# Gated mix of linear-memory attention and a ReGLU block: memory retrieval with phi(Q) stationary, and an order written out per engine

## Chip, cores and metric

One core of one Trainium2 chip. The metric is the device time of one launch in microseconds. The kernel before was run three times: 268.81, 269.09 and 269.09 us, median 269.09.

## What is computed

Inputs are x (2048 tokens by 512, bf16), attention weights wq, wk, wv, wo (512 by 512), one gate beta per head, the weights of a ReGLU block (512 by 1792 twice, 1792 by 512), and a gate vector. Attention has 32 heads of 16 and works in 4 segments of 512 tokens; a memory M (16 by 16 per head) and a denominator vector z are carried from segment to segment.

```python
phi = lambda t: jnp.where(t > 0, t + 1.0, jnp.exp(t))
for s in range(N):                       # 4 segments of 512 tokens
    p = softmax(qs @ ks.T * scale + mask)
    a_dot = p @ vs
    num = einsum('bhld,bhde->bhle', phi(qs), M)
    den = einsum('bhld,bhd->bhl', phi(qs), z) + 1e-06
    o = g * num / den + (1.0 - g) * a_dot         # g = sigmoid(beta), per head
    M = M + einsum('bhld,bhle->bhde', phi(ks), vs)
    z = z + phi(ks).sum(over tokens)
a = o @ wo
b = (relu(x @ W_gate) * (x @ W_up)) @ W_down
out = gx * a + (1 - gx) * b                       # gx = sigmoid(sum(x * gate_w)), per token
```

In segment 0 the memory is empty, so retrieval (num and den) is computed in segments 1 to 3 only.

## The kernel before

**Data.** Activations lie transposed: `xT`, `QT`, `KT`, `pqT` (phi of Q) and `oT` have features on 128 partitions, in 4 blocks of 128 features (8 heads each), and 512 tokens along the row. The hidden layer `hT` has 14 blocks. All weights stay in SBUF. `xT` is double-buffered; segments 1 to 3 are brought in by a DMA transpose on the sync queue (SP, L352). The buffer `xT[1]` first serves to stage segment 0, which TensorE (PE) transposes itself (L404).

**Attention in a segment.** For each pair of feature blocks nine QK steps (L738) each fill the four banks of the PSUM tile `sp`; ScalarE (ACT) takes the exponential (L749) and GpSimd (POOL) masks the diagonal (L759). A step PV (L808) multiplies with the values for one feature block; VectorE (DVE) transposes the result 32 by 32 (L826), takes the reciprocal of the softmax sums (L831), multiplies with gates (L834) and with the product (L837), adds the memory's part (L842) and transposes back into `oT` (L859).

**Memory.** For a finished segment, phi(K) is transposed by DMA (`pkT` to `pK`, L352 as well), multiplied with the values (L650), accumulated in `mzacc`, and spread into `mnum` (a block-diagonal 128 by 128 per feature block) and `mden` (128 by 8) by L668 and L671. In the next segment:

- ZD (L687): 16 matmuls with a tile of phi(Q) as weights and 8 columns of `mden` streaming give the denominators, tokens on partitions. DVE adds 1e-6 (L694) and takes the reciprocal (L697); POOL multiplies with the gates (L700, L703) and copies the result into the layout `coefM` in 48 small copies (L711).
- MR (L779): one matmul per feature block with `mnum` as weights and 512 columns of phi(Q) streaming gives the numerators, features on partitions. DVE transposes them (L786), DVE or POOL multiplies with `coefM` (L792), and the sum with the softmax part follows in L842.

**The rest.** Per segment 14 pairs of gate and up products (L918) with relu (L930 or L932) and product (L937), then four output rows of down product (L952) and wo (L965) in the same bank, scaled out of PSUM (L974 or L976) and stored. The last output row is cut into three column pieces (L876, L884). The head gates are computed once, near the start, by L434 to L437.

**PSUM banks.** Apart from `sp` there are four banks `rb`, shared by all other products: a step takes a bank, and the step that reads it out gives it back.

**Order.** All work is recorded as steps in a `Plan`, with engine, cost, latency, dependencies and a due time. `lay_out` walks through modelled time and on each free engine starts the ready step with the smallest due time, shifted by the tables `SHIFT` and `NUDGE`; a bank is chosen in the same walk. The emission order of each engine is the result; on the chip every engine works through its list in order and waits on semaphores. Two DMA issues are moved to another step's place by `issue_with` (L997).

Of the kernel before, what the change touches and what calls it, by code (L numbers as in the profile page):

```python
# [8 lines left out]
BF16 = mybir.dt.bfloat16  # L9
F32 = mybir.dt.float32  # L10
# [24 lines left out]
NCH = 2  # L35

SHIFT = {'PA': 15, 'PB': 0, 'LIKE': 35, 'T': -43, 'PQ': 42, 'N': -104, 'MZ': -228, 'PV': -136, 'OS': -150, 'OC': -94, 'R': -63, 'EX': -241, 'QK': -81, 'KC': 5, 'H': -95, 'KTR': -235, 'TG': -121, 'PK': -281, 'VC': -64, 'MN': 30, 'XC': 118, 'MK': 208, 'K': -25, 'U': 10, 'D': 11, 'EK': 57, 'MQ': 24, 'EQ': -42, 'TR': 201, 'MA': -36, 'KO': 124, 'V': -15, 'G': 8, 'QC': 201, 'KX': 50, 'W': 72, 'Q': -21, 'OX': 45, 'TA': -65, 'GS': 41, 'TL': -45, 'TN': 103, 'TB': 8, 'MR': 0}
KEEP = {'D': 2, 'U': 1, 'Q': 2, 'G': 1, 'V': 1, 'MZ': 1}  # L40
SWITCH = 0.094
NUDGE = [
# [57 lines left out]
T0, TU, SPAN, PEN_D, PEN_A, PEN_P = 19.0, 15.6, 4.1, -23.0, 150.0, 146.0  # L100


PORT = {'KO', 'MB', 'MQ', 'MN', 'GS', 'PQ', 'PK', 'N1', 'N2', 'N3', 'NM'}
PIECE = {'MK': 0.445, 'TL': 0.22, 'ZE': 0.24, 'YL': 0.22, 'MB': 0.3}


# [934 lines left out]
```

## Time and profile before

| what | value |
|---|---|
| runs | 268.81, 269.09, 269.09 us |
| the profiled execution | 268.84 us, of which the span from first to last instruction is 267.1 us |
| busy, share of the span | PE 97%, ACT 72%, DVE 69%, POOL 61% |
| ACT L749 (exponentials) | 72 of 1876 ns |
| POOL L759 (masks) | 256 of 443 ns |
| DVE L937 (hidden product) | 56 of 684 ns |
| DVE L786 (transpose of the retrieved numerators) | 12 of 700 ns |
| DVE L842 and POOL L842 (sum of both parts) | 18 of 428 ns, 6 of 754 ns |
| POOL L711 (copies into `coefM`) | 48 of 243 ns |

An entry "72 of 1876 ns" is a group of instructions of one source line: count and mean length. Lengths of neighbouring instructions on one engine can overlap, because an engine may start one before the one ahead has left its pipeline. A "wait" or "idle before" names what released the engine.

### The profile page before, as it was taken

The page shows a single profiled execution, that of the slowest core. Times are in us where ns is not written, and L with a number is a line of the kernel's source. Part 1 is how long each engine was busy: PE and PEld are TensorE (multiplying, and loading weights), DVE is VectorE, ACT ScalarE, POOL GpSimd, SP SyncE. Part 2 cuts the span into 40 slices and gives each one's busy share as a digit, 9 for nine tenths or more (in the row PEclk, how much of TensorE's full clock was granted, in tenths as well). Part 3 has the DMA queues.
Part 4 walks back from the last instruction along what each step waited for, and adds up shares of the span by engine and source line. Part 5 has one row for each costly group of instructions (what it writes and reads, how often), then busy time and mean ns, then how long its engine had stood idle before and what let it go on. Part 6 is the DMA issues. An engine that isn't in the chain of part 4 may idle for free.

```text
span 267.1 us, 8000 instructions
## 1 busy us (share of the span) xinstructions
PE 258.6 (97%) x3322; PEld 120.8 (45%) x3365; DVE 185.4 (69%) x414; ACT 192.3 (72%) x185; POOL 163.5 (61%) x378
## 2 busy tenths in 40 slices
PE   7999999999999999999999999999999999999995
PEld 5544544444454444444445544444444444444444
DVE  1476898798589956995858758896816545878800
ACT  3789999987789876687978867666559757876021
POOL 8435788557888874644884888644425785645400
PEclk9999999999999999999999999999999999999999
DMA  6996682221203210000210000000020000000011
GB/s 202 338 345 143 119 281 25 46 57 35 51 28 75 49 38 22 2 2 0 59 22 25 21 22 0 23 4 0 2 64 20 25 0 22 0 4 2 2 39 39
DMA packets 26292, 15.06 MB, mean 56 GB/s; under 512 B 13584, under 2 KB 26256, under 8 KB 26256
## 3 DMA queue, kind: packets, MB, share of 16 engines
q1 hardware_dynamic: 25904, 14.29, 19.6%
q8 instruction: 26, 0.43, 0.6%
q10 hardware_dynamic: 288, 0.26, 0.3%
q14 instruction: 10, 0.08, 0.1%
q0 software_dynamic: 64, 0.00, 0.0%
HBM read 8.13 MB, written 2.10 MB: 38 GB/s over the span
## 4 chain that ended last, share of the span: by engine, by line
PE 92%; issue 2%; POOL 2%; DMA 1%; ACT 1%; DVE 1%; SPq 0%; DVEq 0%; POOLq 0%
PE rb L918 36%; PE rb L952 16%; PE rb L491 10%; PE sp L738 9%; PE rb L808 7%; PE rb L965 5%; PE rb L533 4%; DMA wv_sb<-in_A_wv_dram 1%; PE rb L876 1%; PE rb L779 1%; PE rb L516 1%; POOL E L759 1%; ACT E L749 1%; POOL mnum L668 1%; DVE tA L826 0%
## 5 line engine op out<-in xcount | busy, mean ns | idle before, releaser
L749 ACT ACTIVATE E<-sp 128x2048 bf16<-128x2048 f32 x72 | 135.1, 1876 | 34.5 <-PE sp L738 32.9
L759 POOL TENSOR_SCALAR_AFFINE_SELECT E<-E 64x256 bf16<-64x256 bf16 x256 | 113.4, 443 | 74.6 <-ACT E L749 62.3
L918 PE MATMUL rb<-xT,wg_sb 128*128 128x512 bf16 x214 | 55.0, 380 | 0.6
L918 PE MATMUL rb<-xT,wu_sb 128*128 128x512 bf16 x212 | 54.7, 380 | 0.8 <-issue 0.3
L937 DVE TENSOR_TENSOR hT<-rb,rg 128x512 bf16<-128x512 f32 x56 | 38.1, 684 | 23.3 <-PE rb L918 14.6
L952 PE MATMUL rb<-wd_sb,hT 128*128 128x512 bf16 x198 | 47.0, 379 | 1.6 <-issue 1.4
L918 PEld LDWEIGHTS <-wg_sb 128*128 128x128 bf16 x224 | 20.4, 98 | 26.2 <-issue 4.3
L918 PEld LDWEIGHTS <-wu_sb 128*128 128x128 bf16 x224 | 20.6, 98 | 25.2 <-issue 3.0
L952 PEld LDWEIGHTS <-hT 128*128 128x128 bf16 x210 | 19.3, 98 | 24.6 <-issue 3.5
L738 PE MATMUL sp<-QT,KT 16*64 16x320 bf16 (+7 forms) x512 | 30.3, 295 | 0.1
L738 PE MATMUL sp<-QT,KTo 32*64 32x320 bf16 (+7 forms) x512 | 30.3, 295 | 0.0
L930 ACT ACTIVATE rg<-rb 128x512 bf16<-128x512 f32 x35 | 20.8, 595 | 8.8 <-PE rb L918 7.0
L826 DVE STREAM_TRANSPOSE tA<-rb 128x512 f32<-128x512 f32 x32 | 20.8, 689 | 7.0 <-PE rb L808 7.0
L738 PEld LDWEIGHTS <-KT 16*64 16x64 bf16 x512 | 10.6, 102 | 28.3 <-issue 28.3
L974 ACT ACTIVATE osb<-rb,ngcol 128x512 bf16<-128x512 f32 x11 | 7.5, 685 | 15.9 <-PE rb L965 15.9
L808 PE MATMUL rb<-E,Vs 64*32 64x448 bf16 (+7 forms) x512 | 18.8, 284 | 0.0
L808 PE MATMUL rb<-E,Vp 64*32 64x448 bf16 (+7 forms) x512 | 18.4, 284 | 0.0
L491 PE MATMUL rb<-xT,wq_sb 128*128 128x512 bf16 x63 | 16.3, 380 | 0.1
L491 PE MATMUL rb<-xT,wk_sb 128*128 128x512 bf16 x60 | 15.9, 379 | 0.2
L932 DVE TENSOR_SCALAR rg<-rb 128x512 bf16<-128x512 f32 x21 | 14.2, 683 | 1.3 <-PE rb L918 0.7
L965 PE MATMUL rb<-wo_sb,oT 128*128 128x512 bf16 x57 | 14.4, 379 | 0.5 <-issue 0.5
L389 DVE CAST QT<-rb 128x512 bf16<-128x512 f32 x11 | 7.6, 689 | 9.4 <-PE rb L491 9.4
(107 smaller groups left out, 313.9 us busy)
## 6 DMA issues: line engine op xcount, KB each, us to landing
out_dram<-osb SPq DMA_DIRECT2D x15, 128.0 KB, 1.7
wd_sb<-in_B_W_down_dram SPq DMA_DIRECT2D x1, 1792.0 KB, 8.0
wg_sb<-in_B_W_gate_dram SPq DMA_DIRECT2D x3, 512.0 KB, 7.0
wu_sb<-in_B_W_up_dram SPq DMA_DIRECT2D x3, 512.0 KB, 8.5
Vs<-Vp SPq DMA_DIRECT2D x8, 144.0 KB, 3.2
wk_sb<-in_A_wk_dram SPq DMA_DIRECT2D x2, 256.0 KB, 3.9
wq_sb<-in_A_wq_dram SPq DMA_DIRECT2D x2, 256.0 KB, 4.7
wo_sb<-in_A_wo_dram SPq DMA_DIRECT2D x1, 512.0 KB, 8.8
```

What stands on the lines that cost most here:

```text
L491: nc.tensor.matmul(rb[s.bank][:], lhsT=w[:, ci, c * P:(c + 1) * P], rhs=xT[i][:, ci, :], start=(ci == 0), stop=(ci == NC - 1))
L738: nc.tensor.matmul(sp[64 * h:64 * h + 64, j, off:off + m], lhsT=kt[32 * j:hi, c0 + w, 64 * ck:64 * ck + 64], rhs=QT[i][32 * j:hi, c0 + w, ...
L749: nc.scalar.activation(Er[n % NE][:], sp[:], ACT.Exp, scale=SCALE)
L759: nc.gpsimd.affine_select(out=v, in_=v, compare_op=ALU.is_ge, fill=0.0, base=0, pattern=[[0, 4], [1, 64]], channel_multiplier=-1)
L808: nc.tensor.matmul(rb[s.banks[h]][32 * j:32 * j + 32, q0:q0 + m], lhsT=v[64 * h:64 * h + 64, ck // 2, o:o + 32], rhs=Er[(base + f) % NE][6 ...
L826: nc.vector.transpose(tA[k].rearrange("p b w -> p (b w)"), rb[a.banks[r]][:])
L918: nc.tensor.matmul(rb[s.bank][:], lhsT=w[:, ci, fv * P:(fv + 1) * P], rhs=xT[i][:, ci, :], start=(ci == 0), stop=(ci == NC - 1))
L930: nc.scalar.activation(rgb[k][:], rb[a.bank][:], ACT.Relu)
L932: nc.vector.tensor_scalar(rgb[k][:], rb[a.bank][:], 0.0, None, ALU.max)
L937: nc.vector.tensor_tensor(hT[:, fv, :], rb[a.bank][:], rgb[k][:], ALU.mult)
L952: nc.tensor.matmul(rb[b][:], lhsT=hT[:, fv, lc:lc + P], rhs=wd_sb[:, fv, :], start=(fv == 0), stop=False)
L965: nc.tensor.matmul(rb[hold.bank][:], lhsT=oT[i][:, ci, lc:lc + P], rhs=wo_sb[:, ci, :], start=False, stop=(ci == NC - 1))
```

## The change

Retrieval is turned round, and the way the order is made is replaced.

- `mnum` and `mden` become one tile `mem` of 136 columns per feature block. `retrieve` takes the place of `coefficients`: for each of the 16 combinations of 128 tokens and one feature block, the phi(Q) tile is the stationary operand and the 136 columns stream. Numerators and denominators arrive together, tokens on partitions. Six MR steps per segment hold 3, 3, 3, 3, 2 and 2 of these matmuls in one bank each.
- A step RN follows each MR on DVE: add 1e-6, reciprocal, multiply with `gr` (head gate times token gate, one POOL operation per segment), multiply the numerators into `mtok`.
- Four DMA transposes MX per segment on the sync queue bring `mtok` into `memT` (features on partitions).
- The sum with the softmax part is now OA, an addition into `oT` after the second transpose (L859), on DVE or POOL. L786, L792 and L842 are gone; L837 writes `o16` directly.
- `ORDER` lists the steps of each of PE, ACT, DVE, POOL and SP in sequence; `lay_out` follows the lists and still chooses banks. `SHIFT`, `KEEP`, `NUDGE` and `issue_with` are gone. The order on every engine differs from the one before; among other things the transpose of segment 1's x is issued after the first weight load, and relus and evacuations are divided anew between ACT and DVE.
- The first two shifts of V wait for six weight loads, and the load of wo, like that of W_down, waits for segment 0's phi(K) transposes.

```diff
+RW = P + 8
-NUDGE = [
...
+ENGINES = ('PE', 'ACT', 'DVE', 'POOL', 'QSP')
+ORDER = [
...
+        for v in ORDER:
+            queues[ENGINES[v % len(ENGINES)]].append(self.steps[v // len(ENGINES)])
...
+        while len(order) < len(self.steps):
+            best = None
+            for e in line:
+                if at[e] == len(queues[e]):
+                    continue
+                s = queues[e][at[e]]
+                if s.left or s.take > len(free):
+                    continue
+                t = max(free_at[e], s.ready, free[s.take - 1][0] if s.take else 0.0)
+                if best is None or t < best[0]:
+                    best = t, e, s
...
-    mnum = [sb([NC, P], BF16, f"mnum{i}") for i in range(2)]
-    mden = [sb([NC, 8], BF16, f"mden{i}") for i in range(2)]
-    dinv = sb([4, H], F32, "dinv")
-    coefM = [sb([NC, NB, 2], F32, f"coefM{i}") for i in range(2)]
+    mem = [sb([NC, RW], BF16, f"mem{i}") for i in range(2)]
+    gr = sb([4, NC, 8], F32, "gr")
+    rcf = [sb([3, 8], F32, f"rcf{i}") for i in range(2)]
+    mtok = sb([4, D], BF16, "mtok")
+    memT = sb([NC, L], BF16, "memT")
...
+        def z2(e, s):
+            nc.gpsimd.tensor_tensor(gr[:], gcat[:, None, :, 1, :].to_broadcast([P, 4, NC, 8]),
+                                    rcol[:, 4 * seg:4 * seg + 4, None, None].to_broadcast([P, 4, NC, 8]), ALU.mult)
+        g = add(f"ZC{seg}", {"POOL": 0.5}, z2, after=[hrow, d["TE"]] + recs, prio=want - 20.0)
+        d["MX"] = []
+        cuts = (0, 3, 6, 9, 12, 14, 16)
+        for q in range(6):
+            ks = range(cuts[q], cuts[q + 1])
+
+            def mrv(e, s, ks=ks):
+                for n, k in enumerate(ks):
+                    t, c = divmod(k, NC)
+                    nc.tensor.matmul(rb[s.bank][:, RW * n:RW * n + RW], lhsT=pqT[i][:, c, t * P:(t + 1) * P], rhs=mem[o][:, c, :],
+                                     start=(n == 0), stop=(n == len(ks) - 1), skip_group_check=True)
+            mr = add(f"MR{seg}{q}", {"PE": 0.061 * len(ks)}, mrv, after=d["PQ"] + st[seg - 1]["mb"], prio=want + 4.0 * q,
+                     take=True, lat=0.25)
+            d["mr"].append(mr)
+
+            def rn(e, s, ks=ks, mr=mr, q=q):
+                n, f = len(ks), rcf[q % 2]
+                b = rb[mr.bank][:, 0:RW * n].rearrange("p (n w) -> p n w", n=n)
+                nc.vector.tensor_scalar(f[:, 0:n], b[:, :, P:], 1e-6, None, ALU.add)
+                nc.vector.reciprocal(f[:, 0:n], f[:, 0:n])
+                nc.vector.tensor_tensor(f[:, 0:n], f[:, 0:n], gr.rearrange("p t c h -> p (t c) h")[:, ks[0]:ks[-1] + 1], ALU.mult)
+                nc.vector.tensor_tensor(mtok.rearrange("p t (c h v) -> p (t c) h v", c=NC, h=8)[:, ks[0]:ks[-1] + 1],
+                                        b[:, :, 0:P].rearrange("p n (h v) -> p n h v", h=8),
+                                        f[:, 0:n, :, None].to_broadcast([P, n, 8, DH]), ALU.mult)
+            recs.append(add(f"RN{seg}{q}", {"DVE": 0.42 + len(ks) * P / 960.0}, rn,
+                            after=[mr, g] + (st[seg - 1]["MX"] if seg > 1 else []), prio=want + 4.0 * q, give=mr))
             for t in range(4):
+                if ks[0] <= 4 * t + 3 <= ks[-1]:
+                    d["MX"].append(transpose(f"MX{seg}{t}", memT[:, :, t * P:(t + 1) * P], mtok[:, t, :],
+                                             recs[-2:] + oadd[-NC:], want + 4.0 * q, 128))
...
-                chain = [n1, n2, n3, n4] if seg else [n1, n2, n3]
+                chain = [n1, n2, n3]
...
+            if seg:
+                def oa(e, s, c=c):
+                    eng = nc.gpsimd if e == "POOL" else nc.vector
+                    eng.tensor_tensor(oT[i][:, c, :], oT[i][:, c, :], memT[:, c, :], ALU.add)
+                b = add(f"OA{seg}{c}", {"DVE": 0.34, "POOL": (1.1, PEN_P)}, oa, after=[b, *d["MX"]], prio=want, lat=0.2)
+                oadd.append(b)
```

More of the change, by code (lines that the diff above doesn't have):

```diff
@@ L125, in add @@
         kind = name.rstrip("_0123456789") if name[0] != "N" else "N"
-        s.name, s.lat, s.prio, s.emit = name, lat, prio + SHIFT.get(kind, 0.0), emit
+        s.name, s.lat, s.prio, s.emit = name, lat, prio, emit
         s.engines = {e: (c if isinstance(c, tuple) else (c, 0.0)) for e, c in engines.items()}
         s.after = [a for a in after if a is not None]
-        s.take, s.give, s.keep, s.mode = int(take), give, KEEP.get(kind, 0), mode
+        s.take, s.give, s.keep, s.mode = int(take), give, 0, mode
         s.followers, s.start, s.bank, s.which = [], None, None, which
@@ L136, in lay_out @@
     def lay_out(self):
+        line, queues = sorted({e for s in self.steps for e in s.engines}, key=self.first), {}
+        for e in line:
+            queues[e] = [s for s in self.steps if list(s.engines) == [e]] if e not in ENGINES else []
+        for v in ORDER:
+            queues[ENGINES[v % len(ENGINES)]].append(self.steps[v // len(ENGINES)])
         for s in self.steps:
             s.left, s.ready = len(set(s.after)), 0.0
-            s.prio += NUDGE[s.seq] / 10.0 if NUDGE else 0.0
@@ L140, in lay_out @@
             for a in set(s.after):
                 a.followers.append(s)
-        waiting = [s for s in self.steps if s.left == 0]
-        events = [(0.0, -1, None, None)]
-        n = 0
-        free_at = {e: 0.0 for s in self.steps for e in s.engines}
-        now, done, order, mode = 0.0, 0, [], "full"
-        pool = sorted(self.banks)
-        gp, lock = (0.0, 0.0, 99.0), 0.0
-        while done < len(self.steps):
-            if not events:
-                raise RuntimeError("plan stuck: " + ", ".join(s.name for s in waiting[:8]))
-            now = events[0][0]
-            while events and events[0][0] <= now + 1e-9:
-                _, _, what, s = heapq.heappop(events)
-                if what == "done":
-                    if s.give is not None:
-                        pool.extend(s.give.banks[n_] for n_ in s.which or range(len(s.give.banks)))
-                    for f in s.followers:
-                        f.left -= 1
-                        if f.left == 0:
-                            waiting.append(f)
-            going = True
-            while going:
-                going = False
-                for e in free_at:
-                    if free_at[e] > now + 1e-9:
-                        continue
-                    best = held = None
-                    here = []
-                    for s in waiting:
-                        if e in s.engines:
-                            key = (s.prio + s.engines[e][1] - (SHIFT.get("LIKE", 0) if e == "PE" and s.mode != "full" != mode else 0.0), s.seq)
-                            if not s.take or len(pool) >= s.keep + s.take:
-                                here.append((key, s))
-                            elif s.take > 1 and (held is None or key < held):
-                                held = key
-                    for key, s in here:
-                        if held is not None and s.take and key > held:
-                            continue
-                        if best is None or key < best_key:
-                            best, best_key = s, key
-                    if best is None:
-                        continue
-                    waiting.remove(best)
-                    best.start = (now, len(order), e)
-                    if best.take:
-                        best.banks = [pool.pop(0) for n_ in range(best.take)]
-                        best.bank = best.banks[0]
-                    cost = best.engines[e][0]
-                    if e == "PE":
-                        cost += SWITCH if best.mode != mode else 0.0
-                        mode = best.mode
-                    if e == "DVE" and best.port:
-                        if now < gp[1]:
-                            rest = min(gp[0] + (int((now - gp[0]) / gp[2]) + 1) * gp[2], gp[1]) - now
-                            cost += max(0.0, rest - 0.14)
-                        lock = now + cost
-                    elif e == "POOL":
-                        cost += max(0.0, lock - now)
-                        gp = (now, now + cost, best.piece)
-                    free_at[e] = now + cost
-                    n += 1
-                    heapq.heappush(events, (now + cost, n, "free", None))
-                    n += 1
-                    heapq.heappush(events, (now + cost + best.lat, n, "done", best))
-                    order.append(best)
-                    done += 1
-                    going = True
@@ new lines, in lay_out @@
+        at, free_at = {e: 0 for e in line}, {e: 0.0 for e in line}
+        free = [(0.0, b) for b in self.banks]
+        gp, lock, mode, order = (0.0, 0.0, 99.0), 0.0, "full", []
+        while len(order) < len(self.steps):
+            best = None
+            for e in line:
+                if at[e] == len(queues[e]):
[6 more added lines that the diff above has]
+                    best = t, e, s
+            if best is None:
+                raise RuntimeError("plan stuck")
+            now, e, s = best
+            cost = s.engines[e][0]
+            if s.take:
+                s.banks = [b for _, b in free[:s.take]]
+                s.bank = s.banks[0]
+                del free[:s.take]
+            if e == "PE":
+                cost += SWITCH if s.mode != mode else 0.0
+                mode = s.mode
+            if e == "DVE" and s.port:
+                if now < gp[1]:
+                    rest = min(gp[0] + (int((now - gp[0]) / gp[2]) + 1) * gp[2], gp[1]) - now
+                    cost += max(0.0, rest - 0.14)
+                lock = now + cost
+            elif e == "POOL":
+                cost += max(0.0, lock - now)
+                gp = (now, now + cost, s.piece)
+            free_at[e] = now + cost
+            done = now + cost + s.lat
+            s.start = (now, len(order), e)
+            order.append(s)
+            at[e] += 1
+            if s.give is not None:
+                for n in s.which or range(len(s.give.banks)):
+                    free.append((done, s.give.banks[n]))
+                free.sort(key=lambda f: f[0])
+            for f in s.followers:
+                f.ready = max(f.ready, done)
+                f.left -= 1
@@ L209, in lay_out, with first @@
         self.order = order
         return max(s.start[0] for s in order)
+    def first(self, e):
+        return next(s.seq * 64 + list(s.engines).index(e) for s in self.steps if e in s.engines)
 def act(n, sbuf=False):
@@ L335, with dma @@
     add = plan.add
[L338 removed]
+    def dma(eng, o, i, after=(), prio=0.0, kb=512, lat=3.0, name="dma"):
         key = {"SP": nc.sync, "ACT": nc.scalar, "POOL": nc.gpsimd}[eng]
@@ L465, in sh @@
                                   in_=Vp[i][64 - 64 * h:128 - 64 * h, :, VR * h:VR * h + VR])
-            d["VS"].append(add(f"VS{seg}{h}", {"QSP": 0.65}, sh, after=d["V"] + prev, prio=t_unit(seg, 0) - 2.0, lat=2.2))
+            d["VS"].append(add(f"VS{seg}{h}", {"QSP": 0.65}, sh, after=d["V"] + prev + ([ld[f"{w}{n}"] for w in ("wg", "wu") for n in range(3)] if seg == 0 else []), prio=t_unit(seg, 0) - 2.0, lat=2.2))
     def t_unit(seg, c):
@@ L677, in memory, with retrieve @@
         d["mb"] = [add(f"MB{seg}", {"DVE": 0.95, "POOL": (2.05, 60.0)}, mb, after=[m] + rd, prio=want)]
-    def coefficients(seg):
+    def retrieve(seg):
         i, d, o = seg % 2, st[seg], (seg - 1) % 2
-        want = t_unit(seg, 0)
-        def zd(e, s):
-            for t in range(4):
-                for c in range(NC):
-                    nc.tensor.matmul(rb[s.bank][:, H * t + 8 * c:H * t + 8 * c + 8], lhsT=pqT[i][:, c, t * P:(t + 1) * P],
-                                     rhs=mden[o][:, c, :], start=(t == 0 and c == 0), stop=(t == 3 and c == NC - 1),
-                                     skip_group_check=True)
-        z = add(f"ZD{seg}", {"PE": 16 * 0.027}, zd, after=d["PQ"] + st[seg - 1]["mb"], prio=want, take=True, lat=0.25)
-        d["mr"].append(z)
-        def z0(e, s):
-            nc.vector.tensor_scalar(dinv[:], rb[z.bank][:, 0:4 * H].rearrange("p (t h) -> p t h", t=4), 1e-6, None, ALU.add)
-        def z1(e, s):
-            nc.vector.reciprocal(dinv[:], dinv[:])
-        def z2(e, s):
-            nc.gpsimd.tensor_tensor(dinv.rearrange("p t (c h) -> p t c h", c=NC),
-                                    dinv.rearrange("p t (c h) -> p t c h", c=NC),
-                                    gcat[:, None, :, 1, :].to_broadcast([P, 4, NC, 8]), ALU.mult)
-            nc.gpsimd.tensor_tensor(dinv[:], dinv[:], rcol[:, 4 * seg:4 * seg + 4, None].to_broadcast([P, 4, H]), ALU.mult)
-        b = add(f"ZA{seg}", {"DVE": 0.25}, z0, after=[z] + (st[seg - 1]["CF"] if seg > 1 else []), prio=want, give=z)
-        b = add(f"ZB{seg}", {"DVE": 0.88}, z1, after=[b], prio=want)
-        b = add(f"ZC{seg}", {"POOL": 0.9}, z2, after=[b, hrow, d["TE"]], prio=want)
-        d["CF"] = []
-        for q in range(4):
-            def z3(e, s, q=q):
-                for j in range(4):
-                    nc.gpsimd.tensor_copy(coefM[i][32 * j:32 * j + 32].rearrange("p c (t q) r -> p c t q r", q=4)[:, :, :, q, :],
-                                          dinv[32 * q:32 * q + 32].rearrange("p t (c h) -> p c t h", c=NC)[:, :, :, 2 * j:2 * j + 2])
-            d["CF"].append(add(f"ZE{seg}{q}", {"POOL": 0.95}, z3, after=[b] + (st[seg - 2]["cr"] if seg > 2 else []), prio=want))
@@ L774, in attend @@
                 fill(seg, c)
-            os_, mem = [], []
-            if seg >= 1:
-                def mrv(e, s, c=c):
-                    nc.tensor.matmul(rb[s.bank][:], lhsT=mnum[(seg - 1) % 2][:, c, :], rhs=pqT[i][:, c, :],
-                                     start=True, stop=True)
-                mr = add(f"MR{seg}{c}", {"PE": mm(L)}, mrv, after=d["PQ"][c:c + 1] + st[seg - 1]["mb"] + mems[-2:][:1] * (len(mems) > 1),
-                         prio=tu + 0.8 * TU, take=True, lat=0.25)
-                d["mr"].append(mr)
-                def tm(e, s, mr=mr, u=u):
-                    nc.vector.transpose(tM[u % 2].rearrange("p b r e -> p (b r e)"), rb[mr.bank][:])
-                t = add(f"TM{seg}{c}", {"DVE": dve(L)}, tm, after=[mr] + mems[-2:][:1] * (len(mems) > 1),
-                        prio=tu + 0.8 * TU, lat=0.15, give=mr)
-                def n3m(e, s, c=c, u=u):
-                    eng = nc.gpsimd if e == "POOL" else nc.vector
-                    eng.tensor_tensor(om[u % 2][:], tM[u % 2][:],
-                                      coefM[i][:, c, :, :, None].to_broadcast([P, NB, 2, DH]), ALU.mult)
-                mem = [add(f"NM{seg}{c}", {"DVE": dve(L), "POOL": (1.1, PEN_P)}, n3m,
-                           after=[t, *d["CF"]] + (sums[-2] if len(sums) > 1 else []), prio=tu + 0.85 * TU, lat=0.15)]
-                mems.append(mem[0])
-                d["cr"].append(mem[0])
-            adds = []
+            os_ = []
             want = tu + TU * 0.95
@@ L813, in attend @@
             pp = a = add(f"PV{seg}{c}", {"PE": 1.02}, pv, mode="cols2",
-                         after=[masks[base + f] for f in need] + d["V"] + d["VS"] + mems[-2:][:1],
+                         after=[masks[base + f] for f in need] + d["V"] + d["VS"],
                          prio=want, take=2, lat=0.3)
@@ L859, in t2 @@
                 nc.vector.transpose(oT[i][:, c, :], o16[u % 2].rearrange("p b r e -> p (b r e)"))
-            d["oT"].append(add(f"TB{seg}{c}", {"DVE": dve(L)}, t2, after=os_ + wr, prio=want - 10.0, lat=0.2))
-            otr.append(d["oT"][-1])
-    fills, readers, masks, kph, kts, otr, chains, pvs, mems, sums = [], {}, {}, [], [], [], [], [], [], []
+            b = add(f"TB{seg}{c}", {"DVE": dve(L)}, t2, after=os_ + wr, prio=want - 10.0, lat=0.2)
+            otr.append(b)
+            if seg:
[4 more added lines that the diff above has]
+                oadd.append(b)
+            d["oT"].append(b)
+    fills, readers, masks, kph, kts, otr, chains, pvs, recs, oadd = [], {}, {}, [], [], [], [], [], [], []
     rgn, rgu, sts = [0], [], []
@@ L990 @@
             if seg == 0:
-                ld["wd"].after += st[0]["PK"]
+                for w in ("wd", "wo"):
+                    ld[w].after += st[0]["PK"]
         else:
@@ L995 @@
         st[seg]["readers_xT"] = st[seg]["xr"]
-    def issue_with(step, host, first):
-        own, hosts = step.emit, host.emit
-        step.emit = lambda e, s: None
-        def both(e, s):
-            for fn in (own, hosts) if first else (hosts, own):
-                fn(e, s)
-        host.emit = both
-    issue_with(ld["wu1"], ld_x[1], True)
-    issue_with(ld["wo"], ld["wd"], False)
     plan.makespan = plan.lay_out()
```

31 lines of the change are left out of this document (10 added, 21 removed), and 111 rows, old and new, of tables (NUDGE, ORDER).

## Prediction

> **What bounds the kernel now.** I read the busy shares first, then what TensorE waited for, then the chain that ended last.
>
> ```profile
> PE 258.6 (97%) x3322; PEld 120.8 (45%) x3365; DVE 185.4 (69%) x414; ACT 192.3 (72%) x185; POOL 163.5 (61%) x378
> ```
>
> ```profile
> PE rb L952 <- issue: 1.4, 9, 0.2
> PE rb L394 <- DVE zeros L265: 1.1, 1, 1.1
> PE rb L404 <- DMA xT<-in_A_x_dram: 0.5, 1, 0.5
> PE rb L965 <- issue: 0.5, 3, 0.2
> PE rb L918 <- issue: 0.3, 2, 0.2
> ```
>
> A busy PE alone proves little, because pipelined matmuls overlap. The second view proves it: in 267.1 us PE waited 1.1 us for the first memset, 0.5 us for the first load, and otherwise only for "issue". No wait for VectorE (DVE), ScalarE (ACT) or GpSimd (POOL) is left after the first few microseconds. So the time is the sum of PE's own steps. A microsecond of PE work taken out is worth a microsecond; DVE or POOL work taken out is worth nothing by itself; and whatever makes PE wait is paid in full. The granted clock is 1.00 in every stage.
>
> **PE's work.** These pieces of the chain give the prices (start, length, line, matmuls):
>
> ```profile
> 144.36 0.38 PE rb L687 x16
> ...
> 260.04 1.53 PE rb L876 x14
> ...
> 262.01 0.78 PE rb L876 x14
> ```
>
> L687 (denominators, 8 columns) takes 0.38 us for 16, three times: 1.1 us, removed. L779 (retrieval, 512 columns) has 12 matmuls at 0.216 us, the spacing of the 512-column matmuls (8 in 1.73 us in the same view): 2.6 us, removed. Added are 48 matmuls of 136 columns, each with weights of its own. L876 does just that: a fresh hT tile for each matmul, 0.78/14 = 55.7 ns at 128 columns, 1.53/14 = 109 ns at 256. So 136 columns cost 59 ns, and 48 of them 2.8 us. PE's net is 1.1 + 2.6 - 2.8 = **0.9 us less**. In the built order the changes between full-array and tiled matmuls number 164 in both kernels, so they cancel.
>
> The Trainium skill, "TensorE: Matmul & The Clock Gate", section on the back-to-back issue gap, speaks against this: in a stream of weight loads and matmuls it gives about 81 ns for N=128, and calls the short gap that of an isolated matmul. By it the 48 would take 3.9 us or more and PE would gain nothing. The L876 row, a stream with a load for every matmul, does not agree; I take the row.
>
> **DVE's work, where the change can lose.** Gone from DVE: L786 8.4, L842 7.4, its share of L792 5.1, L697 2.8, L694 0.9: 24.6 us. From POOL: L711 11.7, L792 5.8, L842 4.5, L700 and L703 2.6. None was waited for by PE, so this gains nothing directly. Added on DVE are 18 normalisation steps RN (add 1e-6, reciprocal, times the gate, then the wide multiply out of PSUM) and 10 of the 12 additions OA into oT. The new order also moves work from ACT: relus on DVE go from 21 to 34, output scalings from 5 to 10, Q evacuations from 11 down to 5.
>
> The four operations of an RN depend on one another, and each waits for DVE's own semaphore in the built program. What such a wait costs is visible at the head gates, L434 to L437 (start, length):
>
> ```profile
> 7.46 0.18 DVE L434 TENSOR_SCALAR gbt<-eb 128x32 f32<-128x32 f32 x1
> 7.68 0.35 DVE L435 RECIPROCAL gb<-gbt 128x32 f32<-128x32 f32 x1
> 8.07 0.18 DVE L436 COPY gcat<-gb 128x32 f32<-128x32 f32 x1
> 8.16 0.18 DVE L437 TENSOR_TENSOR gcat<-eb,gb 128x32 f32<-128x32 f32 x1
> ```
>
> L437 needs nothing of L436 and starts 0.09 us after it, inside it. L435 needs L434 and starts 0.22 us after it, 0.04 us behind its end. A dependent operation pays its whole length plus about 0.03 us. The later timeline agrees:
>
> ```profile
> 207.51 0.29 DVE L694 TENSOR_SCALAR dinv<-rb 128x128 f32<-128x128 f32 x1 [1.11 <-PE rb L687]
> 207.84 0.95 DVE L697 RECIPROCAL dinv<-dinv 128x128 f32<-128x128 f32 x1
> 208.71 0.65 DVE L826 STREAM_TRANSPOSE tA<-rb 128x512 f32<-128x512 f32 x1
> ```
>
> L697 starts 0.33 us after L694; the independent L826 starts inside L697.
>
> So an RN on 24 denominators costs: add 0.18 (0.18 at 32 elements in L434), reciprocal 0.29 (between 0.22 at 16 elements in L831 and 0.35 at 32), gate 0.18 (0.19 in L834 and L437), each plus 0.03: 0.74. The wide multiply of 384 PSUM elements lies between L837 (256 elements, 0.38 at the shortest) and L937 (512, 0.69), less the 0.08 that the next instruction overlaps: 0.47. That is **1.2 us**, and by the same rows 1.0 us for the two-piece RN (16 denominators, 256 elements). The plan that the order was built for books 0.42 + 0.13 a piece: 0.82 and 0.69. Its 0.42 fits independent operations, not a chain. Missing: 12 x 0.38 + 6 x 0.31 = 6.4 us. Ends: nothing if the slack holds it all, 6.4 us if each RN releases what PE waits for.
>
> The Trainium skill, "VectorE: DVE Perf Modes", section on the DRAIN, says that the next operation waits for the pipe to empty anyway and that the semaphore costs nothing extra. The rows above do not agree: 0.22 us with the dependence, 0.09 us without. By the page the plan's figure would be right, which is the first rival below.
>
> **Where it bites.** An RN gives back the PSUM bank of its product MR, and only four such banks exist. At the turn from segment 0 to 1 the built order has on PE: MR (2 matmuls), MR (3), MR (3), the second half of a down product (L952, 7), MR (2), a QK, then three K projections (L491, 4 matmuls each). The down product holds one bank throughout, so the last MR needs the first RN's bank and the three K projections need those of the second, third and fourth. On DVE stand RN, a small reciprocal, RN, RN, a small multiply, RN. Counting from the first MR, PE wants the first K at 0.12 + 0.18 + 0.18 + 7 x 0.216 + 0.12 + 0.45 = 2.6 us. DVE starts at about 0.4 (0.22 matmul length in the L876 row, the second matmul, a semaphore), so the second RN ends at 0.4 + 1.0 + 0.15 + 1.2 = 2.75, and its bank is free at about 2.95 (0.08 of tail, 0.1 of semaphore): 0.35 late. The second K is wanted at 2.95 + 0.93 = 3.9, free at 4.15: 0.25. The third is wanted at 5.0, free at 0.4 + 1.0 + 0.15 + 1.2 + 1.2 + 0.1 + 1.0 + 0.2 = 5.25 to 5.3: 0.3. Together **0.9 us**. With the plan's figures the fourth RN ends at 3.85 and nothing is late. The order decides at a mean RN of about 0.88 us; I have 1.1, the plan 0.75.
>
> Five other RNs stand directly ahead of a product that takes their bank or share its queue (one just before this place, two around the last QK blocks of segment 2, two in segment 3): 5 x 0.38 = 1.9 us at stake. DVE in such stretches is already full (busy 9.67 of 10 us from 50 to 60, 17.3 of 20 from 160 to 180), so I take half: **1.0 us**, bounds 0 and 1.9.
>
> **DMA and the rest, at nothing.** Twelve DMA transposes MX join the sync queue (SP), like the present pK ones: 1.2 us of issue, 2.7 us (2.3 to 4.2) to landing. OA waits for them and the output product W for OA. Between the last PV and the first W of the last segment stand five products of PE, 6.8 us, over a DVE chain of about 5; without that cover an OA is 0.4 us late. SP's first transpose of x moves ahead of all weight loads but one, and the second K product of PE after the first QK now needs it.
>
> ```profile
> xT<-in_A_x_dram SPq DMA_TRANSPOSE x3, 5.5
> ```
>
> The three took 3.9, 5.5 and 9.0 us, the 9.0 behind queued weights. It can start at about 8.3, when its staging tile has been read (last L404), and is wanted at about 15.6: it lands at 12.2 to 17.3. I take 0, since only one 256 KB weight load stands ahead of it; at most 1.7 us late. Weight loads that now stand behind pK transposes have several QK blocks of 3 us before their use.
>
> **Sum.** 268.84 (this profiled execution: span 267.1 and 1.7 around it) - 0.9 + 0.9 + 1.0 = 269.8. The runs' median is 0.25 above the profiled run, so I say **269.9 us**.
>
> **Rivals.**
> - *The RNs cost what the plan says, or slack hides them*: only PE's gain is left, 268.84 - 0.9 = 267.9. This is the other side, faster. It decides at the bank hand-over above, at a mean RN below 0.88 us. For it: PE in the kernel before, laid out by the same kind of plan, waits for nobody. Against it: the L434 to L437 rows. The DRAIN section of "VectorE: DVE Perf Modes" in the Trainium skill would give this result.
> - *The new matmuls do not stream*: if each 98 ns weight load (the L876 load row) is exposed, 48 x 98 = 4.7 us replaces 2.8, so PE has 1.0 more instead of 0.9 less, and with the RN waits 271.7. The page on TensorE in the Trainium skill leans this way; the L876 spacing is against it.
> - *The early transpose is late*: 1.7 on top, 271.5.
> - *The RN excess reaches PE in full*: 268.84 - 0.9 + 6.4 = 274.3, from 271.5 up.
>
> **Chances.** Forecast (268.6 to 271.2) 0.55; RN cheap or hidden (267.5 to 268.5) 0.23; exposed weight loads 0.05; late transpose 0.07; excess in full 0.10. The range from 267.6 to 272.0 leaves out most of the last case and a little of the others. A measurement here can tell about 0.2%, 0.54 us, from no change. Faster by more (under 268.55) is the second case, 0.23; within it (to 269.63) is the low part of the forecast, 0.17; slower is the rest, 0.60.
>
> **What would show it.** Right: L687-like small matmuls gone, the new MR at about 59 ns spacing, the RN chain with 0.03 us gaps and 1.0 to 1.2 us a step, and PE's waits naming DVE (the RN multiply) ahead of K projections at 65 to 72 us. Wrong: RN steps under 0.9 us, PE with no wait for DVE, MR spacing near 98 ns, or a wait of the first segment-1 projection for the DMA of xT.

## The result and the profile after

The changed kernel takes 270.47 us (median of 6 runs, 270.07 to 270.70), the kernel before 268.92 us on the same chip (6 runs, 268.72 to 269.09). The ratio is 1.0056, with a 95% interval of 1.0043 to 1.0069: slower by about 0.6%. The profiled execution took 270.44 us with a span of 268.7 us. The forecast was 269.9 us, in the right direction and 0.6 us short.

The busy shares of the profile after:

```profile
PE 261.7 (97%) x3353; PEld 121.2 (45%) x3353; DVE 189.7 (71%) x462; ACT 184.3 (69%) x175; POOL 140.4 (52%) x319
```

POOL lost 23 us of work and ACT 8, DVE gained 4, and none of this says anything about the time. PE's busy time can't be compared across the two pages either: before, 43 matmul records are missing beside the 3365 weight loads, here none. What PE waited for tells more (in total, times, longest, in us), in the kernel after:

```profile
PE rb L473 <- DVE mtok L690: 1.2, 3, 0.5
...
PE rb L882 <- DVE mtok L690: 0.4, 1, 0.4
PE rb L678 <- DVE mtok L690: 0.4, 1, 0.4
```

The lines left out are waits for the first memset and the first loads (1.8 us in all). Before, PE waited for nobody after the start (the view stands in the prediction). Now three lines name L690, the wide multiply that ends a step RN and gives its PSUM bank back: K projections (L473), a hidden product (L882) and a retrieval product MR (L678). PE's timeline shows the first of them, at the turn from segment 0 to 1 (start, length, line, matmuls, idle time before):

```profile
66.48 0.65 PE L678 MATMUL rb<-mem,pqT 128*128 128x136 bf16 x8
66.97 1.67 PE L916 MATMUL rb<-wd_sb,hT 128*128 128x512 bf16 x7
68.48 0.28 PE L678 MATMUL rb<-mem,pqT 128*128 128x136 bf16 x2
...
69.65 1.02 PE L473 MATMUL rb<-xT,wk_sb 128*128 128x512 bf16 x4 [0.54 <-DVE mtok L690]
71.08 1.02 PE L473 MATMUL rb<-xT,wk_sb 128*128 128x512 bf16 x4 [0.41 <-DVE mtok L690]
72.32 1.02 PE L473 MATMUL rb<-xT,wk_sb 128*128 128x512 bf16 x4 [0.21 <-DVE mtok L690]
```

This is the order that the prediction worked with: four MR, a down product that holds one bank, and three K projections, each of which must wait for the RN of the bank it takes. DVE's timeline of the same stretch (left out: the third RN's reciprocal and the first three operations of the fourth, 71.14 to 71.81):

```profile
66.81 0.17 DVE L687 TENSOR_SCALAR rcf<-rb 128x16 f32<-128x16 f32 x1
67.02 0.25 DVE L688 RECIPROCAL rcf<-rcf 128x16 f32<-128x16 f32 x1
67.31 0.27 DVE L689 TENSOR_TENSOR rcf<-rcf,gr 128x16 f32<-128x16 f32 x1
67.61 0.42 DVE L690 TENSOR_TENSOR mtok<-rb,rcf 128x256 bf16<-128x256 f32 x1
67.96 0.24 DVE L794 RECIPROCAL co<-tA 128x16 f32<-128x16 f32 x1
68.14 0.18 DVE L687 TENSOR_SCALAR rcf<-rb 128x24 f32<-128x24 f32 x1
68.36 0.30 DVE L688 RECIPROCAL rcf<-rcf 128x24 f32<-128x24 f32 x1
68.70 0.31 DVE L689 TENSOR_TENSOR rcf<-rcf,gr 128x24 f32<-128x24 f32 x1
69.04 0.56 DVE L690 TENSOR_TENSOR mtok<-rb,rcf 128x384 bf16<-128x384 f32 x1
69.52 0.17 DVE L687 TENSOR_SCALAR rcf<-rb 128x24 f32<-128x24 f32 x1
...
70.06 0.38 DVE L689 TENSOR_TENSOR rcf<-rcf,gr 128x24 f32<-128x24 f32 x1
70.47 0.56 DVE L690 TENSOR_TENSOR mtok<-rb,rcf 128x384 bf16<-128x384 f32 x1
70.95 0.17 DVE L797 TENSOR_TENSOR co<-co,Gs 128x16 f32<-128x16 f32 x1
...
71.84 0.42 DVE L690 TENSOR_TENSOR mtok<-rb,rcf 128x256 bf16<-128x256 f32 x1
```

In this stretch each operation of an RN starts 0.03 to 0.04 us after the end of the one ahead (66.81 + 0.17 = 66.98, next 67.02). Independent neighbours overlap: L794 starts at 67.96, inside L690, which ends at 68.03. From their first start to the start of what follows, the four RNs took 1.15, 1.38, 1.43 and 1.05 us. The three releases of PE (69.65, 71.08, 72.32) follow the ends of the second, third and fourth L690 (69.60, 71.03, 72.26) by 0.05 to 0.06 us: DVE sets PE's pace here.

**How the stalls are counted.** The idle times in brackets begin at a matmul's modelled end, but starts can be compared across kernels. In what follows a *stall* is the spacing from a matmul's start to the next beyond the shortest spacing that the same pair of steps shows in any of these traces, summed from 11.5 us on. (A pair that only one kernel has can show no stall this way; the wait view has to serve for those.) The kernel before has 0.00 us. The kernel after has 2.68 us: 0.43 at the MR that starts at 61.29, 1.56 at the three K projections, 0.09 near 181.6, and 0.60 at hidden products at 224 to 226. Taking the stall away from the stretch from the first QK to the last matmul leaves 248.52 us before and 247.32 us after. So PE's own work fell by 1.2 us and its waits grew by 2.7 us; the difference of 1.5 us is what the runs show (270.47 - 268.92 = 1.55).

### The profile page after: what moved, and what is told of

Same layout as the page of the kernel before. It is cut to its first block, busy times and chain, and to the rows that moved or that the text cites. A ratio compares the mean times of both kernels' runs of the same rounds, so it can differ in the third digit from the quotient of the medians.

```text
span 268.7 us, 8009 instructions
## 1 busy us (share of the span) xinstructions
PE 261.7 (97%) x3353; PEld 121.2 (45%) x3353; DVE 189.7 (71%) x462; ACT 184.3 (69%) x175; POOL 140.4 (52%) x319
## 4 chain that ended last, share of the span: by engine, by line
PE 91%; DVE 6%; DMA 2%; issue 1%; SPq 0%; DVEq 0%
PE rb L882 35%; PE rb L916 17%; PE rb L473 10%; PE sp L723 9%; PE rb L771 7%; PE rb L929 5%; PE rb L515 4%; DMA wv_sb<-in_A_wv_dram 2%; DVE mtok L690 1%; PE rb L840 1%; PE rb L498 1%; PE rb L678 1%; DVE rcf L688 1%; DVE rcf L689 1%; PE rb L632 1%
## 5 line engine op out<-in xcount | busy, mean ns | idle before, releaser
L744 POOL TENSOR_SCALAR_AFFINE_SELECT E<-E 64x256 bf16<-64x256 bf16 x256 | 111.3, 435 | 91.6 <-ACT E L734 78.3
L882 PE MATMUL rb<-xT,wg_sb 128*128 128x512 bf16 x224 | 56.0, 380 | 0.4 <-DVE mtok L690 0.4
L882 PE MATMUL rb<-xT,wu_sb 128*128 128x512 bf16 x224 | 55.9, 380 | 0.0
L916 PE MATMUL rb<-wd_sb,hT 128*128 128x512 bf16 x210 | 49.9, 380 | 0.0
L882 PEld LDWEIGHTS <-wg_sb 128*128 128x128 bf16 x224 | 20.5, 98 | 25.2 <-issue 4.1
L882 PEld LDWEIGHTS <-wu_sb 128*128 128x128 bf16 x224 | 20.2, 98 | 25.1 <-issue 4.9
L896 DVE TENSOR_SCALAR rg<-rb 128x512 bf16<-128x512 f32 x34 | 23.1, 679 | 6.6 <-PE rb L882 6.2
L789 DVE STREAM_TRANSPOSE tA<-rb 128x512 f32<-128x512 f32 x32 | 22.1, 701 | 7.9 <-PE rb L771 7.3
L894 ACT ACTIVATE rg<-rb 128x512 bf16<-128x512 f32 x22 | 12.8, 598 | 9.2 <-PE rb L882 9.2
L473 PE MATMUL rb<-xT,wk_sb 128*128 128x512 bf16 x64 | 16.3, 379 | 1.2 <-DVE mtok L690 1.2
L473 PE MATMUL rb<-xT,wq_sb 128*128 128x512 bf16 x64 | 16.3, 380 | 0.0
L938 ACT ACTIVATE osb<-rb,ngcol 128x512 bf16<-128x512 f32 x6 | 4.1, 686 | 17.2 <-PE rb L929 17.1
L371 DVE CAST Vp<-rb 128x256 bf16<-128x256 f32 (+1 forms) x18 | 8.4, 474 | 10.5 <-PE rb L515 9.3
L929 PE MATMUL rb<-wo_sb,oT 128*128 128x512 bf16 x60 | 15.3, 380 | 0.0
```

What stands on the lines that cost most here:

```text
L473: nc.tensor.matmul(rb[s.bank][:], lhsT=w[:, ci, c * P:(c + 1) * P], rhs=xT[i][:, ci, :], start=(ci == 0), stop=(ci == NC - 1))
L744: nc.gpsimd.affine_select(out=v, in_=v, compare_op=ALU.is_ge, fill=0.0, base=0, pattern=[[0, 4], [1, 64]], channel_multiplier=-1)
L789: nc.vector.transpose(tA[k].rearrange("p b w -> p (b w)"), rb[a.banks[r]][:])
L882: nc.tensor.matmul(rb[s.bank][:], lhsT=w[:, ci, fv * P:(fv + 1) * P], rhs=xT[i][:, ci, :], start=(ci == 0), stop=(ci == NC - 1))
L894: nc.scalar.activation(rgb[k][:], rb[a.bank][:], ACT.Relu)
L896: nc.vector.tensor_scalar(rgb[k][:], rb[a.bank][:], 0.0, None, ALU.max)
```

## The experiments

The theory is that of the prediction: the RN is a chain of dependent operations on DVE, longer than the plan booked, and PE pays where banks are handed over. Rivals: the chain costs nothing by itself and PE is slower for another reason (weight loads, the transposes, the new order as a whole); or the added DVE work as such is the price.

| kernel | RN with 24 / 16 denominators, us | stall, us | median (runs), us | ratio to before (95%) |
|---|---|---|---|---|
| after | 1.36 / 1.07 | 2.68 | 270.47 (6) | 1.0056 (1.0043 to 1.0069) |
| without the chain | 0.85 / 0.63 | 0.00 | 267.73 (6) | 0.9952 (0.9939 to 0.9966) |
| one more link | 1.58 / 1.30 | 4.36 | 272.35 (4) | 1.0127 (1.0114 to 1.0141) |
| one link fewer | 1.03 / 0.84 | 0.44 | 268.30 (10) | 0.9975 (0.9964 to 0.9985) |
| retrieval spread out | 1.24 / 1.08 | 0.19 | 268.05 (5) | 0.9963 (0.9951 to 0.9975) |
| RN's booked cost alone | 1.36 / 1.05 | 2.58 | 270.46 (5) | 1.0050 (1.0037 to 1.0063) |
| spread, one link fewer | 1.02 / 0.83 | 0.29 | 268.23 (7) | 0.9966 (0.9952 to 0.9980) |
| spread, MR twice | 1.24 / 1.05 | 0.08 | 270.78 (5) | 1.0064 (1.0050 to 1.0077) |

RN lengths are means, from the first operation's start to 0.08 us before the end of the wide multiply, where a follower can start. The kernel before took 268.92 to 268.99 us beside these.

### The same operations without the chain

```diff
-                nc.vector.reciprocal(f[:, 0:n], f[:, 0:n])
-                nc.vector.tensor_tensor(f[:, 0:n], f[:, 0:n], gr..., ALU.mult)
+                nc.vector.reciprocal(rca[q % 2][:, 0:n], one[:, 0:n])
+                nc.vector.tensor_tensor(rcb[q % 2][:, 0:n], one[:, 0:n], gr..., ALU.mult)
...
-                                        f[:, 0:n, :, None].to_broadcast([P, n, 8, DH]), ALU.mult)
+                                        one[:, 0:n, :, None].to_broadcast([P, n, 8, DH]), ALU.mult)
```

> The four operations of each RN are kept at the same shapes, but none reads what another wrote: the reciprocal, the gate and the wide multiply read a constant tile of ones. The normalisation of the retrieved memory is thereby left out. Theory (a dependent DVE operation pays its whole length and 0.03 us, so RN takes 1.2 to 1.4 us and holds its bank): RN falls to 0.8 to 0.9 us start to start, PE's waits for the wide multiply (2.0 us by the wait view, 2.7 us by the starts of its matmuls) go, and the time is 267.8 to 268.4. Rival 1 (the semaphore costs nothing and the number of operations counts): RN stays at 1.2 or more, time 270.2 to 270.7. Rival 2 (the new order itself has the waits, whoever holds the banks): RN falls, but the time stays above 269.5.

Measured: 267.73 us, 0.07 us under the expected range. DVE's timeline in this kernel, one RN and the start of the next:

```profile
67.46 0.12 DVE L690 TENSOR_SCALAR rcf<-rb 128x24 f32<-128x24 f32 x1
67.50 0.29 DVE L691 RECIPROCAL rca<-one 128x24 f32<-128x24 f32 x1
67.70 0.28 DVE L692 TENSOR_TENSOR rcb<-one,gr 128x24 f32<-128x24 f32 x1
67.90 0.55 DVE L693 TENSOR_TENSOR mtok<-rb,one 128x384 bf16<-128x384 f32 x1
68.37 0.17 DVE L690 TENSOR_SCALAR rcf<-rb 128x24 f32<-128x24 f32 x1
```

The reciprocal and the wide multiply are as long as before (0.29 and 0.55 us), but each operation starts inside the one ahead, and the next RN begins 0.91 us after this one instead of 1.38. PE's waits in this kernel:

```profile
PE rb L379 <- DVE zeros L249: 1.1, 1, 1.1
PE rb L919 <- issue: 0.5, 3, 0.2
PE rb L389 <- DMA xT<-in_A_x_dram: 0.3, 1, 0.3
PE rb L932 <- issue: 0.3, 2, 0.2
```

No wait for an RN is left; the one DVE line is the first memset. Count of operations, order, transposes and matmuls are those of the changed kernel, so the dependences alone are worth 270.47 - 267.73 = 2.7 us, and neither the amount of DVE work nor the weight loads nor the DMA moves made the kernel slower. Of the 0.51 us between the two RNs, three links at 0.12 (0.08 of overlap lost, 0.04 of gap) make 0.36, and the gate multiply makes 0.10: it took 0.26 us on average in the changed kernel and 0.15 here. The 0.85 us is also what the plan had booked (0.82).

### One more link

```diff
                 nc.vector.reciprocal(f[:, 0:n], f[:, 0:n])
+                nc.vector.tensor_scalar(f[:, 0:n], f[:, 0:n], 1.0, None, ALU.mult)
```

> One more small operation in every RN, a multiplication by 1.0 that depends on the reciprocal; the result is the same. Theory: each RN is 0.21 us longer (0.18 and 0.03). At the turn from segment 0 to 1 four RNs stand in a row, so the K projections there come 0.8 us later; the RN before them adds 0.2 and the places in segments 2 and 3 add 0.3 to 0.8: time 271.6 to 272.3. Rival 1 (independent of the chain, an operation costs about 0.1 us): 270.8 to 271.2. Rival 2 (PE's waits do not come from RN's length): 270.3 to 270.7.

Measured: 272.35 us, 0.05 over the expected range. An RN grew by 0.22 us, the time rose by 1.9 and the stall by 1.7. PE's waits in this kernel:

```profile
PE rb L473 <- DVE mtok L691: 1.9, 3, 1.0
...
PE rb L883 <- DVE mtok L691: 1.0, 2, 0.6
...
```

The K projections and the hidden products (L883 here) wait longer. 1.7 / 0.22 means that the growth of about 7.5 of the 18 RNs reaches PE; by the runs, 1.9 / 0.22, it is about 8.5.

### One link fewer

`gr` now holds the inverse of both gates, so that the add and the multiplication are one operation and the reciprocal comes last. ACT gets one small exponential per segment for it.

```diff
-                nc.vector.tensor_scalar(f[:, 0:n], b[:, :, P:], 1e-6, None, ALU.add)
+                nc.vector.scalar_tensor_tensor(f[:, 0:n], b[:, :, P:], 1e-6, gr..., ALU.add, ALU.mult)
                 nc.vector.reciprocal(f[:, 0:n], f[:, 0:n])
-                nc.vector.tensor_tensor(f[:, 0:n], f[:, 0:n], gr..., ALU.mult)
```

> RN in three operations: (denominator + 1e-6) times the inverse gate in one operation, reciprocal, wide multiply; POOL computes the inverse gate from 1 + exp(-beta) and exp(-z), for which ACT does one more small exponential per segment. Same order, same plan. Theory: RN is 0.21 to 0.3 us shorter (1.0 us), PE's waits fall from 2.7 to 0.9 to 1.5: time 268.7 to 269.3. Rival 1 (a link costs only about 0.1 us): 269.6 to 270.0. Rival 2 (waits do not come from RN's length): 270.2 to 270.7.

Measured: 268.30 us, below the expected range by 0.4: I had overrated what the shorter RN still costs. One RN in this kernel:

```profile
68.74 0.17 DVE L690 SCALAR_TENSOR_TENSOR rcf<-rb,gr 128x24 f32<-128x24 f32 x1
68.95 0.30 DVE L692 RECIPROCAL rcf<-rcf 128x24 f32<-128x24 f32 x1
69.29 0.56 DVE L693 TENSOR_TENSOR mtok<-rb,rcf 128x384 bf16<-128x384 f32 x1
```

The gaps of 0.04 us are the same, and the RN is 0.33 us shorter in the mean. Of the stall 0.27 us remains at the K projections and 0.17 in segment 3. The four RNs at the turn now average (2 x 1.03 + 2 x 0.84) / 4 = 0.94 us. From there to the 1.25 us of the changed kernel the turn's stall grows by 1.29 us over 0.31 us, about four times the RN's growth; drawn on through these two points, it would be zero at 0.88 us.

### Retrieval spread out, and its parts

The 18 MR, 18 RN and 12 MX steps get other places in the lists, so that fewer RNs stand directly ahead of a product that needs their bank; the arithmetic is that of the changed kernel. The plan's cost, which steers the choice of banks, is corrected as well.

```diff
+MOVE = [
+    ("MR12", 253), ("MR14", 254), ("MR11", 470), ("MR13", 266), ("MR15", 356), ("MR10", 356), ("MR20", 529),
...
+        for e, kind in (("PE", "MR"), ("DVE", "RN"), ("QSP", "MX")):
+            moved = {s.name: s for s in queues[e] if s.name[:2] == kind}
+            queues[e] = [s for s in queues[e] if s.name not in moved]
...
-            recs.append(add(f"RN{seg}{q}", {"DVE": 0.42 + len(ks) * P / 960.0}, rn,
+            recs.append(add(f"RN{seg}{q}", {"DVE": 0.82 + len(ks) * P / 960.0}, rn,
```

> The RN is left as it is. Only the places of MR (PE), RN (DVE) and MX (SP) in the lists are changed, so that seldom more than one MR bank is held at a time, and the plan books RN at its real length when it hands out banks. Theory: the RN steps still take 1.2 to 1.4 us, but PE's waits for them fall from 2.7 us to about 0.5: time 268.2 to 268.8. Rival 1 (DVE as a whole is too full in these stretches, so the waits only move to other evacuations): 269.5 to 270.5, with PE waiting for other DVE lines. Rival 2 (the waits are not what costs the time): unchanged, 270.2 to 270.7.

Measured: 268.05 us, under the expected range by 0.15. The turn in PE's timeline of this kernel:

```profile
66.47 0.35 PE L694 MATMUL rb<-mem,pqT 128*128 128x136 bf16 x3
66.87 1.46 PE L932 MATMUL rb<-wd_sb,hT 128*128 128x512 bf16 x6
68.17 0.46 PE L694 MATMUL rb<-mem,pqT 128*128 128x136 bf16 x5
...
68.91 2.94 PE L489 MATMUL rb<-xT,wk_sb 128*128 128x512 bf16 x12
```

The three K projections now run as 12 matmuls without an idle time in brackets. One MR stands before the down product (one of its seven records is missing) and two behind it; the fourth has moved away. By the starts, the whole stall of 0.19 us that is left lies here: the second K projection starts at 69.97, 0.40 us after the matmul ahead. The RN that ends just before it is this one (its first two operations left out):

```profile
69.13 0.33 DVE L705 TENSOR_TENSOR rcf<-rcf,gr 128x16 f32<-128x16 f32 x1
69.49 0.42 DVE L706 TENSOR_TENSOR mtok<-rb,rcf 128x256 bf16<-128x256 f32 x1
```

The RN is still a chain, and hardly shorter (1.24 us), but PE seldom stands behind it. This is the best of all the kernels, 0.4% faster than before and 2.4 us faster than the change.

The corrected cost alone, with the lists as in the change, gives 95 steps other banks:

> The changed kernel with only the booked cost of RN corrected in the plan (0.82 in place of 0.42, and the pieces): the lists stay, but lay_out hands out other banks to 95 steps. Theory (the order, not the choice of banks, makes the waits): within 0.5 us of 270.5. Rival (the banks chosen with the wrong cost make the waits): 268.0 to 269.0.

Measured: 270.46 us, with nearly the same waits as the change (1.2 us at L473, 0.4 at L882; at the MR near 61 the stall is 0.21 at the product behind it instead of 0.43 at the MR). So other banks alone don't help, and the gain of the spread version needs the places in the lists. The places without the corrected cost were not run. Both cures together, the spread lists and the three-operation RN:

> The moved order and the RN of three operations together. Theory: all waits for RN are gone already in the moved order but for 0.2 us, so the two gains do not add: time 267.6 to 268.0, PE's starts without a gap, as in the kernel without the chain (267.73). Rival (a shorter RN is worth its own 4 us of DVE time wherever PE does not wait): below 267.3.

Measured: 268.23 us, over the expected range; its interval overlaps that of the spread version. The two gains do not add, since both remove the same stall, of which the spread left 0.19 us.

### The price of the new matmuls

```diff
-                for n, k in enumerate(ks):
+                for n, k in [*enumerate(ks), *enumerate(ks)]:
```

> The moved order, with each MR's matmuls issued twice into the same bank (the second pass overwrites the first; the result is the same). It prices the streaming of 136 columns with fresh weights on a PE that waits for nothing. Theory: 48 x 59 ns = 2.8 us more, 270.7 to 271.1. Rival 1 (in a stream of weight loads and matmuls about 81 ns or more each): 271.9 or more. Rival 2 (PE has slack somewhere that takes it): below 270.3.

In the spread kernel each MR matmul is issued twice. Measured: 270.78 us, in the expected range; 2.73 us more than the spread kernel for 48 more matmuls, or 57 ns each, with stalls of 0.08. In the trace of the change 29 of the 33 spacings between neighbouring MR matmuls are 58 to 60 ns and four 69 to 70, while each weight load takes 98 ns:

```profile
L678 PEld LDWEIGHTS <-pqT 128*128 128x128 bf16 x48 | 3.7, 98 | 3.7 <-issue 1.4
```

A load of 98 ns at a spacing of 59 ns runs beside other work: its length doesn't show in the time.

## Why the prediction was right, and what was off

- **PE's work, 0.9 us less: right.** Measured 1.2 us less by matmul starts; the kernel without the chain gives 268.99 - 267.73 = 1.26 us by the runs (0.9 to 1.6). Whether the 0.3 beyond 0.9 is real is not resolved. The 59 ns held (57 by the runs, 58 to 60 in the trace). By the 81 ns of the Trainium skill, "TensorE: Matmul & The Clock Gate", back-to-back issue gap, the 48 would have taken 3.9 us; the trace does not agree.
- **The RN as a chain, 1.2 and 1.0 us: right mechanism, a little low.** Measured 1.36 and 1.07. Add, reciprocal and gaps came as worked out (0.17, 0.25 to 0.30, 0.03 to 0.04). The gate multiply took 0.258 us on average instead of 0.18 (see the last section), and the wide multiply of 384 elements 0.48 instead of 0.47 to its follower.
- **The turn from segment 0 to 1, 0.9 us: the mis-sized term.** Measured 1.56 us. The mechanism, the order and all three K projections were as described. The sum was made with RNs of 1.0, 1.2, 1.2 and 1.0 us; they took 1.15, 1.38, 1.43 and 1.05, 0.61 us more, of which 0.42 is the gate multiply. (By the sum's own spacing of 0.93 us the third K was wanted at 5.08 and not 5.0, which makes its wait 0.2 and the term 0.8.) The deciding point of 0.88 us a mean RN agrees with the 0.88 drawn from the two kernels above; to the second digit that is chance.
- **Five other RNs, 1.0 us: right within its halves.** Measured 0.43 + 0.09 + 0.60 = 1.1 us, at named places: just before the turn, around the last QK blocks of segment 2, and in segment 3. That half of the 1.9 us would show was a guess that came out.
- **DMA at nothing: right.** Segment 1's x was issued at 8.36 and landed at 13.09 us, wanted at about 15.6 (in the kernel before it landed at 22.56). The MX took 2.8 us to landing (2.3 to 4.6), and PE never waited for an OA.
- **The sum.** The kernel before took 268.92; 1.2 less work and 2.7 of waits make 270.4, and 270.47 was measured. The forecast had 0.9 less and 1.9 of waits. Of the 0.6 us between, the turn gives 0.66 and the other RNs 0.12, and PE's larger gain takes 0.3 back. The last step of the forecast does not follow from its reason: 269.8 and the 0.25 us between profiled run and median make 270.1, not 269.9.
- **The rivals.** "The RNs cost what the plan says" would have been 267.9; the kernel without the chain shows exactly that case at 267.73, and that it isn't this kernel. The rule of the Trainium skill, "VectorE: DVE Perf Modes", section on the DRAIN, that the semaphore costs nothing extra falls with it: the same four operations take 0.85 us independent and 1.36 us dependent, and that difference is 2.7 us of kernel time. The same section also says that the next operation waits until the pipe is empty, and that one which isn't held starts earlier; the independent operations here start 0.08 to 0.09 us before the end of the one ahead. Were the wait for the empty pipe the rule for all four, an RN would take its full lengths in either case, 0.18 + 0.29 + 0.18 + 0.55 = 1.2 us by the prediction's rows. So the section gives the plan's 0.82 us only where that wait is set aside, which the prediction doesn't say. Exposed weight loads fall by the 57 to 59 ns. The late transpose did not occur. The excess in full fell, as the length of about 7.5 to 8.5 of the 18 RNs reaches PE and those only beyond their slack.

## What to carry to other kernels

On an in-order engine a chain of small dependent operations must be priced link by link from rows that show the dependence (full length plus 0.03 to 0.04 us here), since rows of independent neighbours hide up to 0.1 us of each. A step that gives back a shared buffer is priced by what stands next in line for that buffer, so fixed lists that put steps of 1.36 us, booked at 0.82, directly ahead of the next users of their banks turned a saving of 1.2 us into a loss of 1.5 here. The cure can be in the places rather than in the arithmetic: moving the retrieval steps away from the front of their banks' next users won back about as much as removing a link, and the two did not add.

## What the runs showed of the hardware that I had not expected

The gate multiply L689 (two small operands in SBUF) varies from 0.18 to 0.40 us at the same shape, with one case of 0.63. The kernel before had the like: L834, from whose mean the prediction took 0.19 us, ran from 0.11 to 0.39, and its four longest (0.37 to 0.39) each ended 0.02 to 0.03 us after a POOL operation that was running. Beside the DVE timeline above stands POOL's (start, length):

```profile
68.57 1.84 POOL L744 TENSOR_SCALAR_AFFINE_SELECT E<-E 64x256 bf16<-64x256 bf16 x4 [0.55 <-ACT E L734]
```

The last of these four masks stands at 70.00 to 70.41, and the gate multiply that starts at 70.06 ends at 70.44; the one that starts at 68.70 ends at 69.01, the mask that began at 68.57 at 68.98. In ten cases in the trace a mask was running when the multiply started. In eight of them the multiply ended 0.02 to 0.03 us after the mask; in the other two the mask had at most 0.1 us left, and the multiply took its usual 0.18 us. With none running it took 0.18 us as well, apart from the one of 0.63 us that stood beside another POOL operation. The add, which reads PSUM, and the reciprocal kept their lengths. In the five other traces that have this multiply, a mask that would outlast it held it in 25 of 28 cases; in the other three the multiply kept its length and the mask took 0.45 to 0.47 us instead of its usual 0.41. So it looks as if a small operation on DVE and a mask on POOL can hold each other up without any semaphore. No experiment took the masks away, so this is a coincidence in time, seen many times over, and its cause was not tested. The lengthening accounts for 18 x (0.258 - 0.18) = 1.4 us of DVE time, of which the turn had 0.09 + 0.13 + 0.20 = 0.42. The multiply of 0.33 us in the spread kernel, the last one that PE stands behind, is another such case: the mask beside it ran from 69.02 to 69.44 us.
